# Turning row tiles by DMA, storing row results from ScalarE, and copying streamed units later in a fused feed-forward and recurrent-attention kernel

## The chip, the cores and the metric

The kernel runs on one core of one Trainium2 chip. The metric is the device time of one execution in microseconds. Five engines run side by side, each with its own instruction queue: TensorE (PE in the profile, its weight loads are PEld), VectorE (DVE), ScalarE (ACT), GpSimd (POOL) and SyncE (SP). DMAs are issued from the queues of SP, ACT and POOL and are carried by the core's 16 DMA engines.

## The reference

All arrays are bf16. `x` has 2048 rows of 1024; there are 64 segments of 32 rows, 32 heads of 128, a memory of 8 rows that each segment hands to the next, and a dense layer of width 3584.

```python
xn = layernorm(x)                              # no scale, no shift, eps 1e-5
# branch A: one segment after the other, 64 in all
mem = mem0                                     # [8, 1024]
for s in range(64):
    h = concat([mem, xn[32*s : 32*s+32]])      # 40 rows
    q, k, v = h @ Wq, h @ Wk, h @ Wv           # 32 heads of 128 each
    p = softmax(mask(q @ k.T * 128**-0.5))     # memory columns are open, the rest causal
    o = (p @ v) @ Wo                           # [40, 1024]
    mem, outs[s] = o[:8], o[8:]
# branch B: dense
f = gelu(xn @ w1 + b1) @ w2 + b2
return x + concat(outs) + f
```

## The kernel before

**Two stages.** Branch B is computed first for all rows (up to some 416 us in the profile), then the 64 segments of branch A run one after the other. Branch B leaves its sum `x + f` in DRAM (`R_n`), and the segments add it to their output.

**Branch B in quarters.** The loop `for tg in range(4)` takes a quarter of the rows, 512, as four row tiles of 128. A quarter has two products on TensorE. The first is 28 blocks `fb` of 8 matmuls against `w1` (`first_product`, L497), with the gelu spread over ACT and DVE behind it. The second is, for each row tile `t`, two column halves `nb` of 28 matmuls against `w2` (L618); DVE adds `b2` and the row tile of `x` (L625, L626) in place in the `x` tile.

**What the next quarter needs.** The first product reads `xn` turned, columns on partitions, from `xnT`: two slabs for the two column halves. Before a quarter's second product, the kernel loads the four row tiles of `x` of the next quarter (`load_x`, L344, on SP) and takes their statistics on DVE (`ln_stats`, L384, L386). Then, for each `t`, DVE normalizes one tile of the next quarter (`ln_apply`, L403), and after the second column half `turn_x` turns it: eight PE transposes of 128x128 (`turned`, L412) into one PSUM tile and two copies from it into `xnT` on ACT and DVE (`turned_out`, L417). The buffer of `xn` has two slots. In PE's queue the eight transposes stand behind the 56 matmuls of their row tile, so PE waits there for `ln_apply` where that is late.

**What is stored at the end of a quarter.** `keep_R` (L447) stores a finished row tile to `R_n`; `keep_xT` (L430, L440) stores the turned rows to `rows_d` and `rowsL_d`, and `turn_R` (L484) rearranges `R_n` into `res_d` and `resL_d` by small DRAM-to-DRAM DMAs, 56 for the first quarter. These are on the SP queue in the first two of the four quarters, so they stand between one quarter's end and the `load_x` for the quarter after the next. For the third quarter `turn_R` is on POOL's queue.

**Unit copies.** Branch A needs 64 weight units of 512 KB per segment. 47 are resident and 17 are streamed again in each segment; 15 of these are first copied in DRAM into a contiguous form, `copies` (`fetch`, L246 and L248, names `Wc_...`). Five resident units, `EARLY`, have places of their own and are fetched with them. Both are issued on SP in the first quarter, right after the `load_x` of the second.

**DMA slots.** The built program gives the DMAs of the SP and ACT queues eight completion semaphores in turn. A DMA is issued only when the one that last used its semaphore has landed, so at most eight of them are outstanding, and an instruction that waits holds all behind it on its engine's queue.

**A segment.** It loads its turned rows (`load_x_rows`, L286), its rows of branch B (`res_d`, L1124) and in every fourth segment, those with `s % 4 == 1`, a further tile `resL_d` (L1150) for the rows that were left over. At the end DVE adds them to the product (L1184), which in a segment with left-over rows comes first for the `resL_d` tile. The queue for these loads and for the output stores is set by one line:

```python
loads = nc.scalar if s < EARLY_SEGS else nc.gpsimd
```

In segments 1 to 4, POOL also issues the last quarter's `turn_R`, some instructions after each streamed unit (L486).

Of the kernel before, what the change touches and what calls it, by code (L numbers as in the profile page):

```python
# [24 lines left out]
SEG = 32  # L25
# [23 lines left out]
SCRATCH = 320  # L49
SMALL = 3776  # L50
LEAD = 6
EARLY_SEGS = 5
LEAD_FIRST = 4
SCORES_0 = (6, 6, 6, 5)
SUMS_0 = (4, 4, 4, 4)
# [59 lines left out]
def kernel(  # L115
# [16 lines left out]
    nc = tc.nc  # L132
# [60 lines left out]
    for j in range(4):  # L193
# [11 lines left out]
        out=m, in_=m, pattern=[[1, NX]], compare_op=ALU.is_ge, fill=0.0, base=0, channel_multiplier=-1,  # L205
    )
    for half in range(2):
        m = mask_left[0:SEG, :, 8 - 8 * half:16 - 8 * half]
        nc.gpsimd.affine_select(
            out=m, in_=m, pattern=[[-8, GRP], [0, 8]], compare_op=ALU.is_ge, fill=0.0, base=0, channel_multiplier=1,  # L210
        )
        nc.gpsimd.affine_select(
            out=m, in_=m, pattern=[[8, GRP], [1 if half else 0, 8]], compare_op=ALU.is_ge, fill=0.0,
# [13 lines left out]
    EARLY = list(low) + ["spare0", "spare1"]  # L227
    RES_PLACES = EARLY + ["xt0", "xt1"] + [f"w1_{k}" for k in range(2, NP1)]
    for k in range(7):
# [7 lines left out]
    copies = {  # L237
        unit: dram.tile([P, 2048], BF16, name="Wc_" + "_".join(map(str, unit)))[:, :]
        for unit in reversed(ORDER) if IS_STREAMED[unit] and unit not in KEPT
    }  # L240

    def fetch(t, unit):
        w, i, u = unit
        if w == "O":
            h = 4 * i + 2 * u
            nc.sync.dma_start(out=t.rearrange("p (h d) -> p h d", d=DM), in_=Wo_v[:, h:h + 2, :])  # L246
        else:
            nc.sync.dma_start(out=t, in_=W_v[w][:, i, 2048 * u:2048 * u + 2048])  # L248

    def fetch_resident(*places):  # L250
        for place in places:
            unit = UNIT_AT[place]
            res_tiles[unit] = slab(place)[:, :]
            fetch(res_tiles[unit], unit)
# [75 lines left out]
    NT = S // P  # L330
    with tc.tile_pool(name="ma", bufs=2) as ma, tc.tile_pool(name="mps", bufs=6, space=PSUM) as mps:
# [31 lines left out]
        for j in range(4):  # L363
            nc.sync.dma_start(
                out=o_sb[32 * j + NX:32 * j + 32, 0:8, :],
                in_=mem0[:, 256 * j:256 * j + 256].rearrange("m (h e) -> m h e", h=8),
# [4 lines left out]
        for i in range(14):  # L371
            t = slab(f"w2_{i}")[:, :].rearrange("p (c d) -> p c d", d=DM)
# [28 lines left out]
        def ln_apply(tt):  # L401
            xn = ma.tile([P, DM], BF16, name="ln_xn")
            nc.vector.tensor_scalar(  # L403
                out=xn[:, :], in0=xtoks[tt], scalar1=mv[:, tt, 0:1], scalar2=rstd[:, tt:tt + 1],
                op0=ALU.subtract, op1=ALU.mult,
            )
            return xn
# [14 lines left out]
        def turn_x(tt, xn, xnT):  # L422
            pT = turned(xn)
            for half in range(2):
                turned_out(tt, pT, half, xnT, nc.scalar.copy if (tt + half) % 2 else nc.vector.tensor_copy)

        def keep_xT(tg, xnT):
            xl = [t[:, 0:512].rearrange("p (g k i t) -> p g k i t", g=2, k=KT, i=GRP) for t in ko_flat]
            for half in range(2):
                nc.sync.dma_start(  # L430
                    out=rows_d[16 * tg:16 * tg + 16, :, 128 * half:128 * half + 128].rearrange("s p c -> p s c"),
                    in_=xnT[half].rearrange("p s k t -> p s (k t)"),
                )
                for g in range(4):
                    nc.gpsimd.tensor_copy(
                        out=xl[g // 2][:, g % 2, 4 * half:4 * half + 4, :, :],
                        in_=xnT[half][:, 4 * g:4 * g + 4, :, NX:SEG].rearrange("p i k t -> p k i t"),
                    )
            for k in range(2):
                nc.sync.dma_start(  # L440
                    out=rowsL_d[4 * tg + 2 * k:4 * tg + 2 * k + 2, :, :].rearrange("g p c -> p g c"),
                    in_=xl[k][:, :, :, :, :].rearrange("p g k i t -> p g (k i t)"),
                )

        def keep_R(ttg, rsb):
            eng = nc.scalar if ttg >= NT - 4 else nc.sync
            eng.dma_start(out=R_n[ttg * P:ttg * P + P, :], in_=rsb[:, :])  # L447

        def main_row(slot):
# [43 lines left out]
        xnT = new_xnT(0)  # L493
# [50 lines left out]
        for tg in range(4):  # L544
# [18 lines left out]
            for fb in range(FC):  # L563
# [3 lines left out]
                else:  # L567
# [4 lines left out]
                    out=xb[:, :], in_=ps[:, :], func=ACT.Identity, bias=b1col[:, fb:fb + 1], scale=1.0  # L572
# [4 lines left out]
                    out=u[:, :], in0=u[:, :], scalar1=0.044715, scalar2=1.0, op0=ALU.mult, op1=ALU.add  # L577
# [20 lines left out]
            if not last:  # L598
                xnT = new_xnT(tg + 1)
                for t in range(4):  # L600
                    xtoks[4 * tg + 4 + t] = load_x(4 * tg + 4 + t)
                if tg == 0:
                    for unit, c in copies.items():
                        fetch(c, unit)
                    fetch_resident(*EARLY)
                for t in range(4):
                    ln_stats(4 * tg + 4 + t)
                ln_sqrt(4 * tg + 4, 4 * tg + 8)
                ln_rstd(4 * tg + 4, 4 * tg + 8)
                for t in range(4):  # L610
                    ttg = 4 * tg + t
                    xn = ln_apply(ttg + 4)
                    rsb = xtoks[ttg]
                    for nb in range(2):
                        cs = slice(nb * 512, (nb + 1) * 512)
                        ps = mps.tile([P, 512], F32, name="ps")
                        for fc in range(FC):
                            nc.tensor.matmul(  # L618
                                ps[:, :],
                                lhsT=gts[fc // 4][:, fc % 4, t * P:(t + 1) * P],  # L620
                                rhs=w2_sb[fc // 2][:, fc % 2, cs],
                                start=(fc == 0),
                                stop=(fc == FC - 1),
                            )
                        nc.vector.tensor_tensor(out=ps[:, :], in0=ps[:, :], in1=b2bc[:, cs], op=ALU.add)  # L625
                        nc.vector.tensor_tensor(out=rsb[:, cs], in0=ps[:, :], in1=rsb[:, cs], op=ALU.add)  # L626
                        if nb == 1:
                            turn_x(ttg + 4, xn, xnT)
                    keep_R(ttg, rsb)
                keep_xT(tg + 1, xnT)  # L630
                for t in range(4):
                    turn_R(4 * tg + t, nc.gpsimd if tg == 2 else nc.sync)
            else:


                start_stream("xn2")
                start_stream("xn3")
                put_mem(o_sb, nxt["hT"], mps.tile([P, 512], F32, name="ps"), wide=False)
                nc.sync.dma_start(out=d_oL[:, 0:DM], in_=Wo_v[:, h + 1, :])
                pss = [mps.tile([P, 512], F32, name="ps") for _ in range(6)]  # L640
                pss += [mps.tile([P, 512], F32, name="pT", bufs=2) for _ in range(2)]
                for n in range(8):
                    cs = slice((n % 2) * 512, (n % 2 + 1) * 512)
                    nc.tensor.matmul(pss[n][:, :], lhsT=ones[0:1, :], rhs=b2row[0:1, cs], start=True, stop=False)
                    nc.tensor.matmul(
                        pss[n][:, :], lhsT=ident, rhs=xtoks[4 * tg + n // 2][:, cs], start=False, stop=False
                    )
                for fc in range(FC):
                    for t in range(4):
                        for nb in range(2):  # L650
                            nc.tensor.matmul(  # L651
                                pss[2 * t + nb][:, :],
                                lhsT=gts[fc // 4][:, fc % 4, t * P:(t + 1) * P],
                                rhs=w2_sb[fc // 2][:, fc % 2, nb * 512:nb * 512 + 512],
                                start=False,
                                stop=(fc == FC - 1),
                            )
                    if fc % 2:
                        fetch_resident(f"w2_{fc // 2}")
                    if fc % 4 == 3:  # L660
                        fetch_resident(f"gT{fc // 4}")
                for n in range(8):
                    cs = slice((n % 2) * 512, (n % 2 + 1) * 512)
                    cp = nc.scalar.copy if n % 2 else nc.vector.tensor_copy
                    cp(out=xtoks[4 * tg + n // 2][:, cs], in_=pss[n][:, :])
                for t in range(4):
                    keep_R(4 * tg + t, xtoks[4 * tg + t])
# [6 lines left out]
    with tc.tile_pool(name="late", bufs=1) as late, \  # L674
# [67 lines left out]
        for s in range(NSEG):  # L742
            g, i4 = divmod(s, GRP)
            first, final = s == 0, s + 1 == NSEG
            loads = nc.scalar if s < EARLY_SEGS else nc.gpsimd
            if 1 <= s <= 4:
# [392 lines left out]
            for n, unit in enumerate(O_UNITS):  # L1139
                t = unit_tile(unit)  # L1140
# [7 lines left out]
                if n == 6 and left_o:  # L1148
                    st["resL"] = pd_main[:, 0:256]
                    loads.dma_start(  # L1150
                        out=st["resL"], in_=resL_d[og, :, :]
# [26 lines left out]
            for w, r in reversed(list(enumerate(tiles))):  # L1178
# [6 lines left out]
                if left_o and not final:  # L1185

                    for b in range(2):
                        c0 = 256 * (2 * b + w)
                        eng = nc.scalar if w else nc.gpsimd
# [66 lines left out]
```

## Time and profile before

| What | Value |
|---|---|
| median of 3 runs | 1818.26 us (1816.41, 1818.26, 4332.87) |
| the profiled execution | 1811.68 us, span 1809.9 us |
| PE busy | 1707.1 us, 94% of the span |
| mean granted TensorE clock | 0.998 |
| DMA, over the span | 592.07 MB, mean 327 GB/s |
| first product of a quarter, second and third quarter | 48.5 us |
| second product, one row tile | 12.09 us |

The span is the time from the first to the last instruction of the profiled execution; 1.8 us of its own time lie outside. Columns of the views: a group has busy time, mean duration in ns, and the engine's idle time before its instructions with what ended it; a row of a timeline has start and duration in us, engine, line, operation, and in brackets the idle time before it. A line such as L618 is a line of the kernel as it is printed above.

### The profile page before, as it was taken

To read this page: it belongs to the slowest core of one execution; us is meant where nothing else is said; L and a number is where in the kernel's file an instruction comes from. 1 tells how busy PE (TensorE), PEld (TensorE's weight loads), DVE (VectorE), ACT (ScalarE), POOL (GpSimd) and SP (SyncE) were. 2 spreads that over 40 slices of the span, in tenths; PEclk is the share of its full clock that TensorE was granted. 3 is DMA by queue.
4 is the path that set the end of the run, shared out by engine and by line. 5 is a ranking of instruction groups with operands and counts; after the bars stand their busy time and mean duration, and the time that the engine had idled before them with its cause. 6 is when DMAs were issued, how large, how long until landed. Compare 5 with 4: busy or idle time off the path is not lost.

```text
span 1809.9 us, 71522 instructions
## 1 busy us (share of the span) xinstructions
PE 1707.1 (94%) x31173; PEld 893.0 (49%) x31173; DVE 978.1 (54%) x2508; ACT 687.9 (38%) x1700; POOL 305.2 (17%) x595
## 2 busy tenths in 40 slices
PE   8999999998988999999999999999999999999997
PEld 4444444444444545545444555554545454555544
DVE  7657483804554555555555555555555555555554
ACT  6334260702333334333333334343433333434333
POOL 0000000411122211111111212111111111111111
PEclk9999999999999999999999999999999999999999
DMA  9931111769999999999999999999999999999997
GB/s 290 308 100 48 52 48 36 246 225 345 385 371 346 389 377 384 387 377 393 380 373 374 383 395 394 368 398 379 393 385 376 382 370 369 398 393 384 391 396 294
DMA packets 220870, 592.07 MB, mean 327 GB/s; under 512 B 46283, under 2 KB 75995, under 8 KB 220556
## 3 DMA queue, kind: packets, MB, share of 16 engines
q1 hardware_dynamic: 197652, 567.08, 83.5%
q0 software_dynamic: 17184, 17.23, 2.9%
q8 instruction: 244, 4.00, 0.9%
q10 hardware_dynamic: 5720, 3.19, 0.6%
q14 instruction: 70, 0.57, 0.1%
HBM read 573.43 MB, written 28.90 MB: 333 GB/s over the span
## 4 chain that ended last, share of the span: by engine, by line
PE 72%; DMA 13%; issue 6%; ACT 4%; DVE 3%; POOL 1%; ACTq 0%; DVEq 0%; POOLq 0%; SPq 0%
PE acc L769 34%; PE acc L1027 12%; PE ps L497 11%; PE ps L618 8%; DMA u<-Wc_O 7%; DMA u<-Wc_V 3%; PE ps L651 2%; ACT mixed L938 2%; PE acc L978 1%; DMA u<-Wc_Q 1%; PE mixed L886 1%; DVE kq L853 1%; DVE pd_main L951 1%; POOL res_d L486 1%; ACT kq L848 1%
## 5 line engine op out<-in xcount | busy, mean ns | idle before, releaser
L769 PE MATMUL acc<-u,hr_home 128*32 128x512 bf16 x11520 | 760.8, 380 | 15.7 <-issue 6.0
L769 PEld LDWEIGHTS <-hr_home 128*32 128x32 bf16 x12288 | 348.0, 96 | 285.5 <-issue 33.8
L769 PE MATMUL acc<-u,hrL 128*32 128x512 bf16 x2880 | 254.5, 380 | 4.4 <-issue 2.4
L497 PE MATMUL ps<-u 128*128 128x512 bf16 (+1 forms) x920 | 194.4, 373 | 2.0 <-ACT u L417 2.0
L267 DVE TENSOR_SCALAR u<-kept 128x512 uint32<-128x512 uint32 x254 | 163.1, 684 | 51.7 <-PE acc L769 39.2
L821 ACT CAST d_oL<-acc 128x512 bf16<-128x512 f32 x143 | 82.0, 585 | 261.0 <-PE acc L769 254.2
L618 PE MATMUL ps<-u 128*128 128x512 bf16 x672 | 147.0, 379 | 0.0
L1027 PEld LDWEIGHTS <-kq 128*32 128x32 bf16 x3908 | 103.1, 96 | 79.0 <-issue 22.2
L1027 PE MATMUL acc<-u,d_oL 128*32 128x512 bf16 x1944 | 133.9, 381 | 8.5 <-DMA u<-Wc_O 4.7
L497 PEld LDWEIGHTS <-u 128*128 128x128 bf16 x920 | 89.8, 98 | 104.9 <-issue 2.4
L1027 PE MATMUL acc<-u,kq 128*32 128x256 bf16 (+1 forms) x2372 | 117.2, 313 | 16.0 <-DMA u<-Wc_O 13.4
L853 DVE STREAM_TRANSPOSE kq<-kq 128x512 bf16<-128x512 bf16 x128 | 91.0, 711 | 74.8 <-ACT kq L848 72.6
L951 DVE TENSOR_TENSOR pd_main<-kq,mixed 128x320 bf16<-128x320 bf16 x128 | 62.4, 487 | 127.3 <-ACT mixed L938 127.3
L848 ACT CAST kq<-acc 128x512 bf16<-128x512 f32 (+2 forms) x192 | 85.3, 444 | 114.7 <-PE acc L769 85.1
L1218 POOL DMA_DIRECT2D out_dram<-hr_home x172 | 87.2, 514 | 227.3 <-DVE hr_home L1184 226.8
L825 ACT CAST kq<-acc 128x512 bf16<-128x512 f32 x128 | 75.2, 587 | 111.2 <-PE mixed L892 109.9
L769 PEld LDWEIGHTS <-hrL 128*32 128x32 bf16 x3072 | 86.3, 96 | 58.1 <-issue 5.9
L916 DVE TENSOR_TENSOR kq<-kq,mixed 128x96 bf16<-128x96 bf16 (+1 forms) x256 | 38.1, 190 | 125.7 <-ACT kq L906 70.5
L618 PEld LDWEIGHTS <-u 128*128 128x128 bf16 x672 | 65.3, 98 | 77.4 <-DVE g_u L579 0.4
L571 ACT ACTIVATE g_xb<-ps,b1col 128x512 bf16<-128x512 f32 x112 | 76.8, 686 | 55.6 <-PE ps L497 54.7
L938 ACT ACTIVATE mixed<-mixed,small_consts 128x160 f32<-128x160 f32 x256 | 94.2, 368 | 8.4
L1027 PEld LDWEIGHTS <-d_oL 128*32 128x32 bf16 x2592 | 63.8, 96 | 63.8 <-issue 16.1
(132 smaller groups left out, 2015.4 us busy)
## 6 DMA issues: line engine op xcount, KB each, us to landing
u<-Wc_K SPq DMA_DIRECT2D x256, 512.0 KB
u<-Wc_V SPq DMA_DIRECT2D x256, 512.0 KB
u<-Wc_O SPq DMA_DIRECT2D x256, 512.0 KB
u<-Wc_Q SPq DMA_DIRECT2D x192, 512.0 KB
u<-in_B_w_dram SPq DMA_DIRECT2D x28, 512.0 KB
u<-in_A_Wq_dram SPq DMA_DIRECT2D x13, 512.0 KB
u<-in_A_Wv_dram SPq DMA_DIRECT2D x12, 512.0 KB
u<-in_A_Wk_dram SPq DMA_DIRECT2D x9, 512.0 KB
```

What stands on the lines that cost most here:

```text
L267: nc.vector.tensor_single_scalar(out=out, in_=in_, scalar=0, op=ALU.bitwise_or)
L497: nc.tensor.matmul(ps[:, SEG * s0:SEG * s1].rearrange("p (s t) -> p s t", t=SEG), lhsT=w1_sb[fb // 2][:, kt, (fb % 2) * P:(fb % 2 + 1) * P ...
L571: nc.scalar.activation(out=xb[:, :], in_=ps[:, :], func=ACT.Identity, bias=b1col[:, fb:fb + 1], scale=1.0)
L618: nc.tensor.matmul(ps[:, :], lhsT=gts[fc // 4][:, fc % 4, t * P:(t + 1) * P], rhs=w2_sb[fc // 2][:, fc % 2, cs], start=(fc == 0), stop=(fc ...
L769: nc.tensor.matmul(o, lhsT=lhs[:, i, :], rhs=m, start=(i == seq[0]), stop=(i == seq[-1]), tile_position=(0, 32 * j),)
L821: cp(out=out, in_=ps.rearrange("p (h e) -> p h e", e=32))
L848: nc.scalar.copy(out=q_home[:, h0:h1, NL:40], in_=ps[:, 32 * h0:32 * h1].rearrange("p (h e) -> p h e", e=32))
L853: nc.vector.transpose(out=home, in_=home)
L938: nc.scalar.activation(out=mixed[:, 160 * b:160 * b + 160], in_=mixed[:, 0:160], func=ACT.Exp, scale=-1.0, bias=off[:, b:b + 1],)
L951: nc.vector.tensor_tensor(out=pdA.rearrange("p c b q -> p b c q"), in0=prA[:, None, :, :].to_broadcast([P, 2, 4, 40]), in1=dd, op=ALU.mult,)
L1027: nc.tensor.matmul(acc[r0:r0 + rows, 0:256 * len(blocks)], lhsT=lhsT, skip_group_check=True, rhs=o_columns(t, k, blocks), start=start, sto ...
L1218: loads.dma_start(out=out_flat[rows, 256 * j:256 * j + 256], in_=res[32 * j:32 * j + NX, :])
```

## The change

Four things change.

- For the second to fourth quarter, three of the four row tiles are no longer turned by PE. A new function `send_x` issues eight DMA transposes on SP for a tile, each of 32 rows by 512 columns, from `xn` straight into `xnT`. They are issued right after `ln_apply`. The first tile of each quarter, `t == 0`, is still turned by PE.
- `keep_R` for the first three row tiles of a quarter goes from SP's queue to ACT's. The fourth stays on SP.
- The 15 unit copies and the five `EARLY` fetches are issued on SP after the second product of the first quarter, between `keep_R` of its last row tile and `keep_xT`, and no longer before that product.
- `EARLY_SEGS` is 7, so the loads and stores of segments 5 and 6 are on ACT's queue.

```diff
-EARLY_SEGS = 5
+EARLY_SEGS = 7
...
+        def send_x(t, xn, xnT):
+
+            for i in range(4):
+                for half in range(2):
+                    nc.sync.dma_start_transpose(
+                        out=xnT[half][:, 4 * t + i, :, :],
+                        in_=xn[SEG * i:SEG * i + SEG, 512 * half:512 * half + 512],
+                    )
+
...
         def keep_R(ttg, rsb):
-            eng = nc.scalar if ttg >= NT - 4 else nc.sync
+            eng = nc.scalar if ttg >= NT - 4 or ttg % 4 < 3 else nc.sync
...
                     xtoks[4 * tg + 4 + t] = load_x(4 * tg + 4 + t)
-                if tg == 0:
-                    for unit, c in copies.items():
-                        fetch(c, unit)
-                    fetch_resident(*EARLY)
                 for t in range(4):
                     ln_stats(4 * tg + 4 + t)
...
                     xn = ln_apply(ttg + 4)
+                    if t > 0:
+                        send_x(t, xn, xnT)
                     rsb = xtoks[ttg]
...
-                        if nb == 1:
+                        if nb == 1 and t == 0:
                             turn_x(ttg + 4, xn, xnT)
                     keep_R(ttg, rsb)
+                if tg == 0:
+                    for unit, c in copies.items():
+                        fetch(c, unit)
+                    fetch_resident(*EARLY)
                 keep_xT(tg + 1, xnT)
```

`NT` is 16, the number of row tiles, and `SEG` is 32. 72 PE transposes become 72 DMA transposes (three quarters, three tiles, eight each); 18 copies out of PSUM go.

## The prediction

> **What bounds the kernel now.** I read the page's row of slices first, to see which engine is full at which stage; then the timeline of PE around a quarter's end, for the price of a turned tile; then SP's and DVE's timelines, for what lies between two quarters; last segment 5.
>
> ```profile
> PE   8999999998988999999999999999999999999997
> DMA  9931111769999999999999999999999999999997
> GB/s 290 308 100 48 52 48 36 246 225 345 385 371 346 389 377 384 387 377 393 380 373 374 383 395 394 368 398 379 393 385 376 382 370 369 398 393 384 391 396 294
> ```
>
> A slice is 45 us. PE is full in all of them. The DMA engines are nearly idle in slices 3 to 7, in which the second to fourth quarter of branch B run, and full in all of branch A. So branch B is a chain on PE, and whatever it gains or loses moves the rest rigidly.
>
> PE at the end of the first quarter:
>
> ```profile
> 97.81 1.89 PE L618 MATMUL ps<-u 128*128 128x512 bf16 x8
> 99.53 0.61 PE L412 MATMUL pT<-hr_home,ln_xn 128*128 128x128 bf16 x8
> 99.98 12.25 PE L618 MATMUL ps<-u 128*128 128x512 bf16 x56
> 112.07 0.61 PE L412 MATMUL pT<-hr_home,ln_xn 128*128 128x128 bf16 x8
> 113.35 3.83 PE L497 MATMUL ps<-u 128*128 128x512 bf16 x17 [0.67 <-ACT u L417]
> ```
>
> Eight transposes delay the next matmuls by 0.45 us (99.53 to 99.98), and at the quarter's end PE waits 0.67 us more for the copies into `xnT`. The row tile itself is 12.09 us.
>
> SP between the first quarter and the loads for the third, from two timelines:
>
> ```profile
> 58.91 2.71 SPq L246 DMA_DIRECT2D Wc_O<-in_A_Wo_dram  x4
> ...
> 83.80 2.65 SPq L248 DMA_DIRECT2D u<-in_A_Wk_dram  x2
> ...
> 114.13 2.55 SPq L430 DMA_DIRECT2D rows_d<-u  x2
> ```
>
> ```profile
> 154.92 0.61 SPq L484 DMA_DIRECT2D resL_d<-R_n  x1
> 155.58 1.87 SPq L344 DMA_DIRECT2D u<-in_A_x_dram  x4
> ```
>
> The unit copies are issued while SP has nothing else to do. From `keep_xT` at 114.13 to the `x` loads at 155.58 SP issues without rest: the 56 small DMAs take 0.64 us each. DVE then uses that `x`:
>
> ```profile
> 164.92 1.28 DVE L384 BATCH_NORM_STATS2 ln_stats<-u 128x6 f32<-128x512 bf16 x2
> ...
> 171.20 0.55 DVE L403 TENSOR_SCALAR ln_xn<-u,ln_mv,ln_rstd 128x1024 bf16<-128x1024 bf16 x1
> ```
>
> From the first statistics to the end of `ln_apply` is 6.8 us (171.75), and PE wants that tile at 173.78. So the loads have room: about 6.4 us at DVE (loads land 2.9 us after issue, by the kernel's first: issued at 0.82, read at 3.68), and 2.0 us at PE.
>
> Segment 5, on DVE, on PE, and by windows:
>
> ```profile
> 567.41 0.42 DVE L1184 TENSOR_TENSOR pd_main<-acc,pd_main 128x256 bf16<-128x256 f32 x1 [4.25 <-DMA pd_main<-resL_d]
> ```
>
> ```profile
> 568.22 4.41 PE L769 MATMUL acc<-u,hr_home 128*32 128x512 bf16 x46 [3.05 <-DVE hr_home L1184]
> ```
>
> ```profile
> 570.00:572.00 2.00, 2.00 (x26) 0.82 (x21) 0.81 (x3) 0.59 (x1) 0.00 (x0) 0.50 0.86 275
> 572.00:574.00 2.00, 2.00 (x60) 1.12 (x56) 0.36 (x1) 0.03 (x1) 0.00 (x0) 0.69 1.02 404
> ```
>
> PE stands 3.05 us for the `resL_d` tile. POOL issued that load at 562.25, after the last quarter's small DMAs; in segment 9 it went out at 646.87, 6.3 us ahead of its use. After the stall the granted clock (the column behind POOL's) is 0.50 and 0.69: about 1.7 us more are lost.
>
> **The change, part by part.**
>
> *Transposes off PE.* Nine tiles by 0.45 us is 4.0 us. Three quarter ends lose the wait of 0.67 us: 2.0 us. Together -6.0 us, if the DMA transposes are in time. The last tile's `xn` is ready 1.6 us after its matmuls begin (101.95 less 99.98, less the copy of 0.41 that goes), and the next quarter's first matmul wants it at 12.1 us. That leaves 10.4 us for eight issues and a landing. No transposing DMA is in the trace. Bounds for its pitch on SP: 0.32 us (the stores of `R_n`) from below, 0.68 us for the unit copies before landings pace them (2.71 / 4), 1.44 us for weight loads of 512 KB that landings pace (11.52 us for eight) from above, and beyond that no row binds it. I take 0.68 us, as the nearest: few bytes, many pieces. 8 x 0.68 + 2.9 = 8.3 us, hidden. The 18 copies out of PSUM go from ACT and DVE, which wait for PE there; worth nothing.
>
> [...]
>
> *Stores of `R_n` on ACT.* ACT waits there for DVE's additions. Queued behind are the two copies of `t == 0` and, 10 us later, the next gelu; ACT sits idle more than 10 us there, so 0. Uncovered it would be 0.45 us an issue.
>
> *Unit copies later.* Where they left, nothing waited for them: 0. In their new place they stand ahead of `keep_xT`, the 56 small DMAs and the `x` loads for the third quarter. They carry 20 x 0.524 = 10.5 MB; at the 318 GB/s of 61 to 96 us in the trace, which is mostly these transfers, 33 us. With eight outstanding, SP gets past them as they land. Counting from the second quarter's start: copies begin at 1.9 us (DVE's last addition and one store); their data is done at 35; `rows_d` queues behind, its first half landing some 4.5 us later, and the fifth small DMA, eight places behind it, can go then, at 39.5; 52 more at 0.64 us and 1.5 us of other waits give the `x` loads at 74 (42 before). They land at 77, `ln_apply` ends at 84. PE reaches its transposes at 48.5 + 12.1 = 60.6. It waits 23 us. Behind it in PE's queue is the whole second product. The clock drops as in segment 5: 2 us. Together +25 us. Bounds: at 400 GB/s, the rate around 560 us, 26 us instead of 33, so +17; at 271 GB/s, the lowest of the windows there, 39 us, so +31. If landings didn't pace SP at all, 20 x 0.32 = 6.4 us of issue just fit the room, and it is 0. I take 25, since `L248 <- DMA` waits stand in SP's list of waits already.
>
> *Segments 5 and 6 on ACT.* In segment 1 ACT issued the `resL_d` load at 467.89, 5.7 us ahead of the cast that opens the segment's end; DVE waited 0.54 us and PE not at all. So segment 5's stall goes: 3.05 + 1.7 = -4.7 us. Bounds: -5.6 (segment 6 took 25.65 us against 20.0 for its like later) and 0 (ACT's load lands as late as POOL's did). Segment 6's four stores cost 2 us on ACT, at a place where it waited 6.2 us for PE.
>
> *Sum.* -6.0 + 25 - 4.7 = +14.3 us. From the profiled execution's 1811.7 that is 1826; the runs' median, 1818.3, lies 6.6 us above it, and the forecast is for that median: 1832.6, say 1832 us.
>
> **The rivals.**
>
> *SP gets past the copies in time* (not slower). The mechanism is one: SP's pace over the 20 moved DMAs. Under about 8 us it delays nothing, and what is left is -6.0 - 4.7: 1807.6 us. For it: an issue alone is 0.32 us. Against: the copies took SP from 58.91 to 86.45 the first time, and `Wc` waits are in its list.
>
> *Transposes a little late.* The pitch is that of the paced weight loads, 1.44 us. 1.6 + 8 x 1.44 + 2.9 = 16.0 us against 12.1: 3.9 us late at each of three ends, without backlog, as a tile's eight (11.5 us) still fit 12.1. That adds 11.7: 1844 us. It begins at a pitch of 0.95 us.
>
> *Transposes far too slow* (slower by over 2%). Beyond 1.5 us of pitch a tile's eight no longer fit its matmuls, and the three tiles queue up. At 2.0 us: 1.6 + 24 x 2.0 + 2.9 = 52.5 us from the second tile's start against 36.3, 16 us late, three times, with 2 us of slow clock each: 54 us more, so 1886 us. At 1.75 us 10 us late each, 1869. For it: nothing bounds the pitch. Against: 32 KB each, and an idle DMA system.
>
> **How the numbers follow.** Forecast 0.55, a little late 0.16, far too slow 0.17, in time 0.12. About 2% (36 us) is what a measurement of this kernel can tell from no change. The forecast, the first and the second rival lie within it; the third mostly above. Nothing summed here reaches 36 us of gain. So faster 0.02, within 0.79, slower 0.19. The range goes from the "in time" case with its own scatter, 1804, over both bounds of the copies and a late transpose, to the near edge of the slow case, 1869. The forecast's own range is 1824 to 1843.
>
> **What would show it.** Right: PE idle some 23 us in the second quarter, between its first and second row tile, before L412, with DVE's statistics waiting for `x`, and a clock of 0.5 behind it; no gap at the three quarter ends; segment 6 at 20 to 21 us. Wrong: `x` issued by SP before 165; gaps before L497 at the quarter ends (the transposes); a DVE wait on `resL_d` in segment 5 as before. If the total is below 1810 us, the copies did not hold SP; if above 1869, the transposes did it.

## The result, and the profile after

| What | Before | After |
|---|---|---|
| median | 1817.41 us (6 runs, 1816.00 to 1819.32 and one of 4332.87) | 1840.61 us (6 runs, 1827.26 to 1856.28) |
| ratio, 95% interval | | 1.011, 1.0071 to 1.0149 |
| the profiled execution | 1811.68 us, span 1809.9 | 1843.38 us, span 1841.7 |
| mean granted TensorE clock | 0.998 | 0.987 |

The changed kernel is 23.2 us slower by the medians, 8.6 us above the forecast. (The ratio is taken over undisturbed runs of both; it makes the difference 20 us, between 13 and 27.) The page's slices of the changed kernel, 46 us each:

```profile
PE   8997699999899999999999999999999999999988
PEclk9999799999999999999999999999999999999999
DMA  9454121667999999999999999999999999999998
GB/s 289 124 167 137 52 69 49 201 195 270 362 379 379 385 382 389 361 378 372 384 383 373 386 386 382 385 378 394 396 376 398 387 376 376 384 390 390 366 370 311
```

Each digit is a share in tenths, 9 being full. PE was at 8 or 9 in every slice of before; now it falls to 7 and 6 in slices 4 and 5, and the granted clock to 7 in slice 5. The copies' traffic has moved from slice 2 (308 GB/s before, 124 now) to slices 3 and 4 (100 and 48 before, 167 and 137 now). The hole lies in the second quarter. PE's timeline there:

```profile
160.96 12.25 PE L625 MATMUL ps<-u 128*128 128x512 bf16 x56
200.17 1.03 PE L412 MATMUL pT<-hr_home,ln_xn 128*128 128x128 bf16 x8 [26.96 <-DVE ln_xn L403]
200.99 38.89 PE L625 MATMUL ps<-u 128*128 128x512 bf16 x168
239.89 1.02 PE L506 MATMUL ps<-u 128*128 128x512 bf16 x4
241.07 47.64 PE L506 MATMUL ps<-u 128*128 128x512 bf16 x220 [0.16 <-issue]
```

PE reaches its only eight transposes of the quarter at 173.21 and stands 26.96 us for `ln_apply`; behind them the other three row tiles take 38.89 us where the first quarter's take 36.42. The windows show why (the column behind POOL's is the granted clock):

```profile
175.00:200.00 25.00, 0.00 (x0) 0.00 (x0) 6.19 (x14) 0.30 (x1) 0.00 (x0) 0.51 0.23 68
200.00:210.00 10.00, 9.83 (x39) 4.47 (x40) 3.78 (x8) 0.58 (x1) 0.49 (x1) 0.70 0.14 42
210.00:240.00 30.00, 30.00 (x140) 13.45 (x139) 7.65 (x13) 0.00 (x0) 0.70 (x3) 1.00 0.15 39
```

The clock is at 0.51 while PE idles and still at 0.70 in the first 10 us after. What SP did between the end of the copies and the `x` loads, from its timeline, and the second `rows_d` store from a narrower window of it:

```profile
138.40 2.30 SPq L248 DMA_DIRECT2D u<-in_A_Wk_dram  x2
142.18 9.60 SPq L439 DMA_DIRECT2D rows_d<-u  x2
...
189.82 0.61 SPq L493 DMA_DIRECT2D resL_d<-R_n  x1
190.47 1.86 SPq L344 DMA_DIRECT2D u<-in_A_x_dram  x4
```

```profile
142.86 8.92 SPq L439 DMA_DIRECT2D rows_d<-u  x1
```

The `x` loads go out at 190.47, where they went out at 155.58 before. DVE starts on them 2.80 us later:

```profile
193.27 1.29 DVE L384 BATCH_NORM_STATS2 ln_stats<-u 128x6 f32<-128x512 bf16 x2 [29.00 <-DMA u<-in_A_x_dram]
...
199.56 0.55 DVE L403 TENSOR_SCALAR ln_xn<-u,ln_mv,ln_rstd 128x1024 bf16<-128x1024 bf16 x1
```

The end of the first quarter, with 36.42 us of matmuls in one piece where three groups of PE transposes stood, and the group of the transposing DMAs by their line (count; smallest, median and largest duration in ns):

```profile
75.42 36.42 PE L625 MATMUL ps<-u 128*128 128x512 bf16 x168
112.30 1.02 PE L506 MATMUL ps<-u 128*128 128x512 bf16 x4 [0.45 <-issue]
113.48 8.79 PE L506 MATMUL ps<-u 128*128 128x512 bf16 x40 [0.16 <-issue]
```

```profile
L431 SPq DMA_TRANSPOSE u<-ln_xn x72: 1162/1237/2278, 77.4 to 336.3; - x72
```

In segment 5, DVE's wait for the `resL_d` tile, 4.25 us before:

```profile
594.59 0.42 DVE L1195 TENSOR_TENSOR pd_main<-acc,pd_main 128x256 bf16<-128x256 f32 x1 [1.01 <-DMA pd_main<-resL_d]
```

**Where the time went.** From the start of a second product to the next first product, before's trace has 50.97 us in each quarter (62.37 to 113.35, 161.69 to 212.66, 261.01 to 311.98). After: 49.42, 78.93 and 48.97 (62.88 to 112.30, 160.96 to 239.89, 288.55 to 337.52). The first product then has one more gap of 0.16 us. So the turning by DMA saves 1.4 to 1.85 us a quarter, 5 us in all, and the stall costs the second quarter 30 us (78.93 against the 48.97 of the third). 30 less 5 is 25, and the fourth quarter does start 25.5 us later (337.52 against 311.98). From there to the end the two traces differ by another 6 us, half of it before the end of the first segment; other pairs of runs differ there too, as the experiments show.

### The profile page after: what moved, and what is told of

The parts are those of the page before. It is cut to its first block, busy times and chain, and to the rows that moved or that the text cites. A ratio compares the mean times of both kernels' runs of the same rounds, so it can differ in the third digit from the quotient of the medians.

```text
span 1841.7 us, 71481 instructions
## 1 busy us (share of the span) xinstructions
PE 1714.4 (93%) x31101; PEld 897.0 (49%) x31101; DVE 974.9 (53%) x2499; ACT 682.8 (37%) x1691; POOL 300.3 (16%) x586
## 4 chain that ended last, share of the span: by engine, by line
PE 72%; DMA 16%; DVE 4%; ACT 3%; issue 3%; SPq 2%; ACTq 0%; POOL 0%; DVEq 0%; POOLq 0%
PE acc L780 34%; PE acc L1038 12%; PE ps L506 10%; DMA u<-Wc_O 8%; PE ps L625 7%; DMA u<-Wc_V 4%; PE ps L662 2%; SPq L493 2%; PE acc L989 1%; ACT mixed L949 1%; DMA u<-Wc_K 1%; PE mixed L897 1%; DMA hr_home<-res_d 1%; DVE kq L864 1%; DVE pd_main L962 1%
```

## The experiments

The theory: the loss is SP's queue. The `x` loads stand behind the copies, `keep_xT` and the 56 small DMAs, and PE waits for them. The rivals: the loss comes from the turning by DMA (then it stays when the copies alone are moved), or copies late are harmless without the other parts. The first four kernels ran on one chip beside 24 runs of before, median 1812.78 us.

**The copies late, alone.** The kernel before, with only this moved:

```diff
                     xtoks[4 * tg + 4 + t] = load_x(4 * tg + 4 + t)
-                if tg == 0:
-                    for unit, c in copies.items():
-                        fetch(c, unit)
-                    fetch_resident(*EARLY)
...
                     keep_R(ttg, rsb)
+                if tg == 0:
+                    for unit, c in copies.items():
+                        fetch(c, unit)
+                    fetch_resident(*EARLY)
                 keep_xT(tg + 1, xnT)
```

> The kernel before with one thing changed: the copies and EARLY fetches stand after the first quarter's second product. Theory: PE waits at the first turned tile of the second quarter for the late x, 27 us, and then runs 2 to 3 us slower on a cold clock; nothing else moves, so 1844 to 1850 us. Rival (the wait needs the DMA turning, whose 24 issues fill SP before the copies): less than 10 us, so under 1828 us.

1843.69 us, ratio 1.0168 (1.0143 to 1.0193): 30.9 us slower, just under the expected 1844 to 1850. PE's timeline has the same hole, though PE does all the turning here:

```profile
200.62 1.03 PE L412 MATMUL pT<-hr_home,ln_xn 128*128 128x128 bf16 x8 [26.34 <-DVE ln_xn L403]
```

So the moved copies alone cost 30 us; the turning by DMA is not part of the loss.

**The copies back in their old place.** The changed kernel, with the copies issued right after the `x` loads, ahead of the second product:

```diff
                     xtoks[4 * tg + 4 + t] = load_x(4 * tg + 4 + t)
+                if tg == 0:
+                    for unit, c in copies.items():
+                        fetch(c, unit)
+                    fetch_resident(*EARLY)
...
                     keep_R(ttg, rsb)
-                if tg == 0:
-                    for unit, c in copies.items():
-                        fetch(c, unit)
-                    fetch_resident(*EARLY)
```

> The changed kernel with the unit copies and EARLY fetches back ahead of the first quarter's second product; turning by DMA, stores on ACT and segments 5 and 6 stay. Theory (the moved copies hold SP, so the third quarter's x is late): the 27 us stall of PE in the second quarter goes, and of the gain of some 5 us from the turning and 5 us from segment 5 all is kept except at the first quarter's end: the transposes now queue behind the copies on SP until about 86.5 us, and 24 of them at the 1.24 us seen end near 117.5 against 112, 5 to 6 us late. So 1812 to 1815 us. Rival (the DMA turning or the stores on ACT slow the rest, seen in the segments as 8 us that came on top): 1817 to 1825 us, with the segments as long as in the changed kernel.

1821.66 us, ratio 1.0047 (1.0028 to 1.0065): slower than the expected 1812 to 1815, and by its number within the range of the rival, 1817 to 1825. The trace decides: the hole of the second quarter is gone, as the theory had it, but the first quarter ends late. SP's timeline (first two rows) and PE's:

```profile
86.39 1.93 SPq L248 DMA_DIRECT2D u<-in_A_Wk_dram  x2
89.31 31.96 SPq L431 DMA_TRANSPOSE u<-ln_xn  x24
```

```profile
121.36 3.99 PE L506 MATMUL ps<-u 128*128 128x512 bf16 x11 [9.38 <-DMA u<-ln_xn]
```

The first transposing DMA goes at 89.31 instead of 77.42, behind the last copy; 24 of them need 31.96 us, and PE starts as they end, 9.4 us late. So with the turning on SP the old place of the copies costs too: 9.4 us of gap where 5 to 6 were expected, and 1.2 us of slow clock in the product behind it (49.96 us instead of 48.8). Nor do the 5 us expected of segment 5 show in the total; the run with segments 5 and 6 on ACT, alone, takes that up. That the turning or the stores on ACT slow the segments, as the rival has it, is not seen in the kernel with the small DMAs on POOL, below: from the first segment's cast to the last it takes 7.0 and 2.4 us less than before in its two traces.

**The `x` loads ahead of the copies.** The changed kernel, with the third quarter's loads issued just ahead of the copies:

```diff
-                for t in range(4):
-                    xtoks[4 * tg + 4 + t] = load_x(4 * tg + 4 + t)
+                if tg != 1:
+                    for t in range(4):
+                        xtoks[4 * tg + 4 + t] = load_x(4 * tg + 4 + t)
...
                 if tg == 0:
+                    for t in range(4):
+                        xtoks[8 + t] = load_x(8 + t)
                     for unit, c in copies.items():
```

> The changed kernel, with the third quarter's four x loads issued on SP just ahead of the copies instead of after the second quarter's first product. Theory (the order on SP is the cause, not the transfers themselves): no stall in the second quarter, and all gains stay: 1805 to 1810 us, faster than both. Rival (the copies slow the second quarter by their traffic, or the turning slows the segments): 1817 us or more.

1822.54 us, ratio 1.0057 (1.0033 to 1.008): not the gain that was expected, and by its number what the rival forecast. But the rival's cause, a second quarter slowed by the copies' traffic, isn't there: its matmuls take as long as before. The stall before L412 is gone, and another has come at the quarter's end. SP's timeline and PE's:

```profile
192.73 30.70 SPq L431 DMA_TRANSPOSE u<-ln_xn  x24
```

```profile
172.75 36.42 PE L626 MATMUL ps<-u 128*128 128x512 bf16 x168
223.44 16.72 PE L506 MATMUL ps<-u 128*128 128x512 bf16 x66 [14.27 <-DMA u<-ln_xn]
```

The second quarter's own transposing DMAs stand behind the 56 small DMAs, until 192.73. They run back to back, 30.70 / 24 = 1.28 us each, and PE waits 14.27 us for the last. The expectation had moved one item out of SP's queue and forgotten the next one that PE waits for.

**Segments 5 and 6 on ACT, alone.** The kernel before with `EARLY_SEGS = 7`.

> The kernel before with EARLY_SEGS 7 and nothing else. Theory: the wait for the left-over tile in segment 5 goes, with its 1.7 us of slow clock: 4 to 6 us less, 1811 to 1814 us. Rival (the segments are bound by DMA and give the gain back): 1816 to 1818 us, with segment 6 short and later ones longer.

1812.23 us, ratio 0.9987 (0.9962 to 1.0011): no difference that these runs resolve. (The number lies in the theory's 1811 to 1814 only because the runs of before beside it came out lower, at 1812.78.) In its trace segment 6, from DVE's cast in one segment to that in the next, takes 20.55 us instead of 25.65, but its lead over before's trace, 8.75 us at the sixth segment, is 0.9 at the thirty-eighth and 1.6 at the end.

**The small DMAs on POOL.** If SP's queue is the cause, it is enough to take the 56 small DMAs of the first quarter off it. The copies stay late. This and the next three ran beside 27 runs of before, median 1815.38 us.

```diff
-                    turn_R(4 * tg + t, nc.gpsimd if tg == 2 else nc.sync)
+                    turn_R(4 * tg + t, nc.sync if tg == 1 else nc.gpsimd)
```

> Copies where the change has them; the 56 small DMAs of the first quarter are on POOL's queue, no longer on SP's, so nothing of theirs stands ahead of the x loads for the third quarter or of the second quarter's transposes. Theory (the stall is SP's queue: copies, then 56 x 0.64 us, then x): the x loads are issued some 36 us earlier than the changed kernel's 190.47, near 155; no gap in PE before L412, and no gap at the second quarter's end; each of three quarters is 1.5 to 1.8 us shorter than before, and segment 5 loses its wait. Against the kernel before -5 to -10 us, ratio 0.994 to 0.997. Rival (the turned-away small DMAs cost elsewhere, on POOL or as DMA traffic under the second product): ratio 1.00 or above, with PE gaps in the second quarter.

1806.65 us, ratio 0.9959 (0.994 to 0.9979): 8.7 us faster than before. SP's timeline and PE's:

```profile
157.26 1.96 SPq L344 DMA_DIRECT2D u<-in_A_x_dram  x4
175.86 34.38 SPq L431 DMA_TRANSPOSE u<-ln_xn  x24
```

```profile
161.30 12.25 PE L625 MATMUL ps<-u 128*128 128x512 bf16 x54
173.39 0.61 PE L412 MATMUL pT<-hr_home,ln_xn 128*128 128x128 bf16 x8
173.83 36.42 PE L625 MATMUL ps<-u 128*128 128x512 bf16 x165
210.25 1.02 PE L506 MATMUL ps<-u 128*128 128x512 bf16 x4
```

The `x` loads go at 157.26, PE has no hole, and the second quarter's end no gap. The copies are where the change put them, so neither they nor their traffic is a loss by itself; the loss is what SP had to issue after them.

**All turning on PE, with that queue.** As the last, with before's `turn_x` for all four tiles.

```diff
-                    if t > 0:
-                        send_x(t, xn, xnT)
...
-                        if nb == 1 and t == 0:
+                        if nb == 1:
                             turn_x(ttg + 4, xn, xnT)
```

> As e5_turn_r_pool, but all four row tiles are turned by PE as in the kernel before: no DMA transposes. It prices the DMA transposes alone, without copies or small DMAs in their way. Theory (they save PE 9 x 0.45 us and part of the end's wait): 4.5 to 6 us slower than e5_turn_r_pool, and 0 to -5 us against the kernel before (segment 5's wait gone). Rival (given back in branch A, as the transposes free PE before a part that DMA paces): equal to e5_turn_r_pool within 2 us, though the fourth quarter starts 4.5 to 6 us later than there.

1809.61 us, ratio 0.9971 (0.9955 to 0.9986). The traces differ as expected in the three quarters: 50.98, 50.97 and 50.97 us each (62.88 to 113.86, 162.20 to 213.17, 261.51 to 312.48) against 49.37, 48.95 and 48.96 with DMA turning, 5.6 us, less 0.16 in each first product. The medians differ by 3.0 us, between the theory's 4.5 to 6 and the rival's 2, and their intervals overlap, so the total confirms the sign at best. The two traces speak for the rival: the fourth quarter starts 4.6 us earlier with DMA turning (307.88 against 312.48), but the cast at the end of the first segment, L324, comes only 0.4 us earlier (450.31 against 450.71). Part of the loss is a slow clock at the start of the fourth quarter's second product, 0.50 for 5 us (360.88 to 365.88) where the kernel that turns on PE has 1.00, with PE idle for 0.3 us in the 5 us ahead of it. Before's trace has 0.66 there and that of the copies late, alone, which also turns on PE, 0.50, so it isn't bound to the turning. Why it comes stays open.

**All four tiles by DMA.**

```diff
-                    if t > 0:
-                        send_x(t, xn, xnT)
+                    send_x(t, xn, xnT)
...
-                        if nb == 1 and t == 0:
-                            turn_x(ttg + 4, xn, xnT)
```

> As e5_turn_r_pool, but the first row tile of each quarter is turned by DMA as well, so no PE transposes are left in the three quarters. Theory (a transposing DMA takes SP 1.24 us, whatever it waits for): 32 x 1.24 = 39.7 us, of which the first starts some 9.6 us after the product does, so the last lands 2 us after the product's 48.4 us: three late ends of about 2 us, less 0.45 us of PE transposes each, +4 to +6 us against e5_turn_r_pool. Rival (SP has room): -1 to -2 us against it.

1817.40 us, ratio 1.0009 (0.9992 to 1.0026): 10.8 us above the one with three tiles, more than expected, in the direction of the theory. PE at the three quarter ends:

```profile
113.15 48.80 PE L506 MATMUL ps<-u 128*128 128x512 bf16 x224 [2.48 <-issue]
...
213.76 50.22 PE L506 MATMUL ps<-u 128*128 128x512 bf16 x224 [3.47 <-issue]
...
315.98 50.28 PE L506 MATMUL ps<-u 128*128 128x512 bf16 x224 [3.66 <-issue]
```

SP needs 41.5 us for the 32, 1.30 us each and not 1.24, so the ends are 2.5 to 3.7 us late instead of 2; and after the second and third the next first product takes 50.2 us instead of 48.8, with a granted clock of 0.66 in its first 5 us, both times. 9.6 us of gaps and 2.9 of slow clock make 12.5; less 1.35 for the PE transposes saved and the 0.9 of gaps that three tiles had, that explains 10.3 of the 10.8. (The profiled execution of this kernel took 1808.89 us, the least of its twelve, so its trace isn't that of the median.)

**Twice as many DMAs of half the size.**

```diff
-                for half in range(2):
+                for q in range(4):
...
-                        out=xnT[half][:, 4 * t + i, :, :],
-                        in_=xn[SEG * i:SEG * i + SEG, 512 * half:512 * half + 512],
+                        out=xnT[q // 2][:, 4 * t + i, 2 * (q % 2):2 * (q % 2) + 2, :],
+                        in_=xn[SEG * i:SEG * i + SEG, 256 * q:256 * q + 256],
```

> As e5_turn_r_pool, but each tile is turned by sixteen DMAs of 32 rows by 256 columns in place of eight of 32 by 512. Theory A (the 1.24 us are a price per DMA): 19.8 us a tile, 59.5 us for three, which start 9.6 us after the second product does at the earliest: 20 to 25 us late at each of three quarter ends, +60 to +80 us with the cold clock. Theory B (the price goes by the elements turned): 0.62 us each, no difference from e5_turn_r_pool within 2 us.

1896.08 us, ratio 1.045 (1.0427 to 1.0473). The group of that line, and PE at the first quarter's end:

```profile
L431 SPq DMA_TRANSPOSE u<-ln_xn x144: 1159/1230/2062, 76.7 to 391.8; - x144
```

```profile
136.29 1.03 PE L506 MATMUL ps<-u 128*128 128x512 bf16 x2 [25.20 <-DMA u<-ln_xn]
```

Half the bytes, the same 1.23 us (median 1230 ns, 1237 with twice the bytes): here the price went by the DMA and not by the element. (Both pieces have 32 rows, so a price by rows isn't excluded.) The ends are 25.2, 24.9 and 24.8 us late, at the upper edge of what was expected; the total, 89 us above the kernel with eight pieces, is above the expected 60 to 80, as the first products behind the first two stalls take 52.1 and 54.3 us (136.29 to 188.40, 262.27 to 316.60) where 48.5 to 48.8 are usual, with the clock at 0.50 in the first 5 us of both.

**Two queues for the turning.** As with all four tiles by DMA, but one column half's DMAs on ACT:

```diff
-                    nc.sync.dma_start_transpose(
+                    (nc.scalar if half else nc.sync).dma_start_transpose(
```

> As e6_all_four (all four row tiles turned by DMA, small DMAs of the first quarter on POOL), but the four DMAs of one column half are issued on ACT, those of the other on SP. Theory A (the 1.24 us are the issuing queue's): each queue needs 16 x 1.3 = 21 us for its half, both lie inside the second product, no gaps at the three quarter ends and no cold clock there: 10 to 12 us faster than e6_all_four, 1 to 2 us faster than e5_turn_r_pool (three times 0.45 us of PE transposes). Theory B (one unit turns for all queues): the two queues take turns, the pitch over both stays 1.24 to 1.3 us, and the ends are late as in e6_all_four, 2.5 to 3.7 us each.

It ran with the next two beside 21 runs of before, median 1813.70 us: 1867.63 us, ratio 1.0289 (1.0255 to 1.0324). Neither theory had this. The first DMAs of the two queues, from ACT's timeline and from SP's in narrow windows, and SP's waits between 60 and 130 us (total, times, longest):

```profile
71.60 1.29 ACTq L431 DMA_TRANSPOSE u<-ln_xn  x1
76.48 1.18 ACTq L431 DMA_TRANSPOSE u<-ln_xn  x1
81.15 1.18 ACTq L431 DMA_TRANSPOSE u<-ln_xn  x1
```

```profile
74.04 1.29 SPq L431 DMA_TRANSPOSE u<-ln_xn  x1
78.79 1.17 SPq L431 DMA_TRANSPOSE u<-ln_xn  x1
```

```profile
SPq L431 <- DMA u<-ln_xn: 41.0, 6, 14.9
```

In the first row tile the queues alternate, 2.3 to 2.4 us from one issue to the next. In the other three, four of SP's go back to back and then four of ACT's (ACT's start at 95.75, 109.41 and 122.46). At each of the 12 changes between the queues the next issue starts 1.1 to 1.8 us after the end of the other queue's last one. SP's list of waits puts six of them, 41.0 us, down to transposing DMAs; ACT's are not listed. So the 32 take 56 us (71.60 to 127.54) where one queue took 41.5, and PE stood 11.84 and 6.15 us at the first end. What two queues would do without these waits was not tried. The handover does give a number that was missing: 1.2 us of issue and, as an estimate from the 2.35 us between issues, 1.15 us more to the landing.

**Segments 5 and 6 back on POOL, and the best version again.** The kernel with the small DMAs on POOL, with `EARLY_SEGS = 5`, and beside it that kernel as it was.

> As e5_turn_r_pool, but the loads and stores of segments 5 and 6 stay on POOL, as in the kernel before. Theory (segment 5's stall is a delay that lasts): 3 to 6 us slower than e5_turn_r_pool. Rival (what a segment wins is waited for again later, as the trace of e4_segs_alone shows it): within 2 us of it.

> The same text as e5_turn_r_pool, run beside e9_two_queues and e10_segs_on_pool so that these are compared on one chip. Against the kernel before: 0.994 to 0.998, as measured there (0.9959).

1809.41 us, ratio 0.997 (0.995 to 0.999), against 1807.83 us, ratio 0.9957 (0.9939 to 0.9976). The second confirms the first measurement: 5.9 us faster than before, after 8.7. The two differ by 1.6 us, within the rival's 2. Their traces part by 4 us in segment 6 (24.54 against 20.36 us) and still differ by 7.7 at the end, where those of the earlier pair did not. So what segments 5 and 6 are worth over the whole run stays open between nothing and some 4 us.

## Why the prediction was right, and where it was off

**The stall: right in place and mechanism, 5 us too small.** Predicted 23 us before L412 and 2 us of slow clock; measured 26.96 and 2.5 (and 0.4 in the transposes themselves), 30 us by the quarter's length against the 25 taken, inside the 17 to 31 (by its own terms the lower bound is 18: 33 less 26 is 7). By its steps, from the second quarter's start at 112.30: copies begin at 1.4 (said: 1.9); the `x` loads go out at 78.2 (74); DVE starts 2.8 us later (2.9); PE comes at 60.9 (60.6). What is missing is the step at `rows_d`. It was to get its first half through and let the fifth small DMA go at 39.5; the first of them went at 42.4. The second `rows_d` store held SP for 8.92 us in its own issue, and `rowsL_d` 2.7 more. The sum had counted semaphores, not that an issue can grow long. Before's trace already has such a row, in the first quarter:

```profile
46.21 7.85 SPq L430 DMA_DIRECT2D rows_d<-u  x1
```

It is the second store of a pair each time. In the changed kernel's trace it took 8.01 us in the first quarter and 8.92 here, where the DMA engines were full ahead of the pair (a share of 1.0 in the 10 us before it, both times), and 2.25 and 1.86 at the ends of the second and third quarter, where they were nearly idle (a share of 0.14 and 0.17 during the first store). The first store of a pair took 0.37 to 0.56 us throughout. (SP's list of waits puts 8.7 of the 8.92 us down to ACT's gelu. The store doesn't depend on that; ACT's last copy into its slab ended at 77.56.)

**The transposes: size nearly right, with two errors that cancel.** Predicted -6.0 us, measured -5 by the length of the quarters; how much of it lasts to the end of the run isn't shown. The pitch was 1.24 to 1.28 us, not 0.68: nearer to the paced weight loads, 1.44, than to the unit copies that I took as the nearest row. The landing was, by the estimate from the handover of two queues, 1.2 us after the issue's end, not 2.9. With the measured numbers a last tile takes 1.6 + 8 x 1.26 + 1.2 = 12.9 us against 12.1 of matmuls: 0.8 late; the first end shows 0.45 + 0.16, the other two 0.16. The rival "a little late" was to begin at a pitch of 0.95; the pitch was beyond that, and only the shorter landing kept the rival from coming true. The 2 us to spare were in truth none, as the kernel with the fourth tile showed.

These pieces did not go out as fast as plain DMAs: 32 KB in 1.28 us (30.70 us for 24) are 26 GB/s, and the 56 plain small DMAs, of 8 to 64 KB, went out of the same queue every 0.64 us.

**The `R_n` stores on ACT: right, as far as seen.** No run has them alone. In the kernel with the small DMAs on POOL, which has them, PE waits for ACT in none of the three second products.

**Segments 5 and 6: right where it looked, not shown in the total.** The stall of PE in segment 5 is gone, and segment 6 takes 20.57 us (said: 20 to 21). Taken as -4.7 us of total time, it measured -0.6 alone and -1.6 in the other pair, neither apart from 0. The step that failed is the rule that whatever moves early moves the rest rigidly. It didn't hold in every pair: the lead of segment 5 shrank in branch A from 8.75 us to 1.6, and that of the turning from 4.6 us to 0.4 between the fourth quarter and the first segment. Why is not shown.

**The sum.** 30 - 5 - (0 to 2) = 23 to 25 against the measured 23.2 (13 to 27 by the ratio). The forecast's +14.3 was 5 short at the copies, 1 at the transposes and 3 to 5 at the segments; all three errors had one sign. Adding 6.6 us for the distance of the profiled run to the median was right in direction for before and of no help for after, whose profiled run lies 2.8 us above its median.

**The rivals.** "In time" is refuted by the late `x` loads; the prediction's own row spoke against it, since at 0.68 us for each of 15 copies and 0.32 for five loads the issues alone are 11.8 us, more than the 8 of room. "Far too slow" is refuted by quarter ends of 0.6 us and less. With sixteen DMAs a tile the latter came true, since 16 x 1.24 no longer fits 12.1.

## What to carry to other kernels

Before a block of DMAs is moved on an issue queue, list everything that stands behind it at the new place, up to the next thing that somebody waits for, and price each of these; here, sending the 56 least urgent DMAs to another queue turned +23 us into -6 to -9 us. Turning tiles by DMA freed the matmul engine here (1.4 to 1.85 us a quarter, with a gain in the total that isn't clear of noise), but a DMA held its queue for 1.23 to 1.24 us at 32x512 and at 32x256 alike, and two queues took 56 us for what one did in 41.5: use few and large pieces on one queue (none above 32x512 was tried), and keep a reserve at the end of the last one.

## What was not expected of the hardware

- A transposing DMA occupied the issuing queue for 1.23 to 1.24 us (median) whether it turned 32x512 or 32x256 elements; of 32x512, 24 or 32 in a row took 1.28 to 1.33 us each with what lay between.
- A plain store of 512 KB held SP for 8.92 us where the DMA engines had been full before it (a share of 1.0 in the 10 us ahead of the pair), and the same store at two other quarter ends for 2.25 and 1.86 us (a share of 0.14 and 0.17 during the pair's first store).
- Behind PE's stalls of 3.47 and 3.66 us in the trace with all four tiles by DMA the clock was 0.66 in the 5 us after, and the next product took 1.4 us more. Behind one of 2.48 us in the same trace it was 1.00.
- At the start of the fourth quarter's second product the clock was 0.50 for 5 us in the trace with the small DMAs on POOL, with PE idle for 0.3 us in the 5 us ahead of it. The copies late, alone, have 0.50 there too, before's trace has 0.66 and that of all turning on PE 1.00.
